# Giving the last 512 rows of a weight matrix to eight of the sixteen DMA engines, and storing the result with one DMA

## The chip, the cores and the metric

The kernel runs on one core of one Trainium2 chip. The metric is the time of one launch on the device, in microseconds (us). The executions of the kernel before lie between 122.95 and 123.44 us in all rounds of the record, and every kernel here was timed beside runs of the kernel before on the same chip. "Span" is the time from the first to the last instruction in the profile; in the kernel before it is about 2 us shorter than the time of the launch.

The profile shows five engines of the core (PE for matmuls, DVE, ACT, POOL, and SP, which here only issues DMAs) and the busy share of its sixteen DMA engines, which move data between the chip's main memory and the on-chip memory SBUF. The kernel uses SBUF as 128 partitions. The second-last load of w_o leaves sixteen completion records in the trace (113.54 to 116.70 us), a store of 8 rows leaves eight (119.60 to 119.68 us) and one more from its issue (118.94). So a `dma_start` is read here as spread over several DMA engines, with one record for the part that one engine carries, called a *share*.

## The reference

The reference is one decoding step for a batch of 8 rows. The input is normalised, and two branches run on the same normalised rows: attention over the last 1024 positions of a cache, and a feed-forward network (FFN). Their results are multiplied and added to the input:

```python
x  = A_x                                   # 8 x 1 x 512, bf16
xn = layernorm(x)
s  = attention(xn, k_cache, v_cache, wq) @ wo       # wo is 4096 x 512
g  = silu((gelu(xn @ w_gate) * (xn @ w_up)) @ w_down)  # w_gate, w_up 512 x 1792; w_down 1792 x 512
return x + s * g
```

Every weight and every cached row is read once, 47.5 MB in all. The arithmetic for 8 rows is small.

## The kernel before

SP issues all loads in one order: the caches and w_q, then w_gate, w_up, w_down, and at the end w_o in four blocks. Every one of these loads writes all 128 partitions. Of the last block, the last quarter is a DMA of its own, so the load that closes the kernel is small.

```python
# w_down: 1792 rows = 128 partitions x 14 rows, two loads of 7 rows a partition
JF = F // P                                   # 14
JH = JF // 2
wd = B_w_down.rearrange("(p j) d -> p j d", j=JF)
for a in range(2):
    t = slot()[:, 0 : JH * D].rearrange("p (j d) -> p j d", j=JH)
    nc.sync.dma_start(out=t, in_=wd[:, a * JH : (a + 1) * JH, :])
...
for m in range(NM):                           # w_o, four blocks of 1 MB
    load_wo(m, cut=HS if m < NM - 1 else HS - 2)   # the last one in 6/8 and 2/8
```

The FFN finishes before the last blocks of w_o arrive. The result sits in PSUM as four column groups of 128; group `q` has the 8 rows of the batch on partitions 32q to 32q+7. Four small DMAs store it, two issued by SP and two by ACT:

```python
def project_out(m):
    for e in range(HS):                       # 8
        for q in range(NQ):                   # 4
            nc.tensor.matmul(s_ps[32 * q : 32 * q + B, :], oE[m][:, e, :],
                             wo_t[m][:, e, q * P : (q + 1) * P], ...)
...
nc.vector.tensor_tensor(out=tmp, in0=s_ps, in1=g_sb, op=ALU.mult)
nc.vector.tensor_tensor(out=out_sb, in0=tmp, in1=xr_sb, op=ALU.add)
for q in range(NQ):
    eng = nc.sync if q % 2 == 0 else nc.scalar
    eng.dma_start(out=out_flat[:, q * P : (q + 1) * P], in_=out_sb[32 * q : 32 * q + B, :])
```

The softmax here doesn't subtract the row's maximum and nothing guards it: scores larger than these inputs give would overflow.

## Time and profile before

| | before |
|---|---|
| time, median (range, 4 runs) | 123.21 us (123.14 to 123.26) |
| span | 121.1 us |
| last share of the second-last w_o load lands | 116.70 us |
| first store issued | 118.47 us |
| last store lands | 120.29 us |

The page of the kernel before: the span, the mean busy share of the DMA engines in 40 equal slices (in tenths), the GB/s in the same slices, two of the queues (packets, MB, share of the sixteen engines' time), and the shares of the chain of waits that ended last.

```profile
span 121.1 us, 4123 instructions
...
DMA  3999999999999999999999999999999999999820
GB/s 84 387 430 430 430 427 417 419 430 425 425 427 427 425 414 422 430 419 430 425 427 422 422 417 430 422 425 422 425 433 418 422 414 434 416 430 423 341 88 5
...
q1 hardware_dynamic: 6800, 47.46, 93.7%
q8 instruction: 14, 0.23, 0.7%
...
DMA 82%; PE 12%; DVE 2%; SPq 1%; issue 0%
```

The kernel is bound by loading: from the third slice to the 37th the engines move 414 to 434 GB/s. The third-last and second-last slices (341, 88) show that the loads do not end together. Queue q8, which the page labels "instruction", has 14 packets of 16 KB in the whole run.

The end of the chain of waits of the kernel before, in order of time. The columns are the start in us, the duration in us, and what it was.

```profile
98.97 17.74 DMA slot<-in_A_wo_dram
116.70 0.04 issue
116.75 1.05 PE s_ps L383 x31
117.80 0.02 issue
117.82 0.30 DVE tmp L483
118.12 0.02 issue
118.14 0.29 DVE out_sb L485
```

So the second-last load of w_o sets the time: when it has landed, at 116.70 us, only about 1.8 us of work and the stores remain. The timeline around it (start in us, length in us, engine, line, what was written and read, and in brackets the idle time before and what ended it):

```profile
108.52 1.12 PE L437 MATMUL m_ps<-slot,hT_sb 128*8 128x128 bf16 x56 [0.55 <-DVE m_ps L433]
...
116.75 1.02 PE L383 MATMUL s_ps<-slot,oE_2360 128*8 128x128 bf16 x32 [0.88 <-DMA slot<-in_A_wo_dram]
...
118.47 0.71 SPq L488 DMA_DIRECT2D out_dram<-out_sb  x2
118.47 0.65 ACTq L488 DMA_DIRECT2D out_dram<-out_sb  x2
```

The completion records say more than the landing time of the whole load. These are the sixteen of the second-last load of w_o, before the change, in us; the trace does not name the engine of a record:

```
113.54 113.55 113.57 113.58 113.77 113.85 114.14 114.42 | 114.97 115.00 | 116.42 116.50 116.53 116.65 116.67 116.70
```

Eight shares end early, two about 1 us later, six about 2.5 us later. That is the opportunity that the change is after. It can be read together with queue q8: each of the 14 instruction packets takes about 0.94 us in its packet record (0.88 to 0.97). Against the mean of the eight early records (113.80 us) the two are 1.2 us late and the six 2.8 us. If an instruction packet sets the later shares of one engine back by 1.2 to 1.4 us, six shares set back twice and two set back once make 14. That is an estimate from these counts.

### The profile page before, as it was taken

To read this page: it belongs to the slowest core of one execution; us is meant where nothing else is said; L and a number is where in the kernel's file an instruction comes from. 1 tells how busy PE (TensorE), PEld (TensorE's weight loads), DVE (VectorE), ACT (ScalarE), POOL (GpSimd) and SP (SyncE) were. 2 spreads that over 40 slices of the span, in tenths; PEclk is the share of its full clock that TensorE was granted. 3 is DMA by queue.
4 is the path that set the end of the run, shared out by engine and by line. 5 is a ranking of instruction groups with operands and counts; after the bars stand their busy time and mean duration, and the time that the engine had idled before them with its cause. 6 is when DMAs were issued, how large, how long until landed. Compare 5 with 4: busy or idle time off the path is not lost.

```text
span 121.1 us, 4123 instructions
## 1 busy us (share of the span) xinstructions
PE 86.0 (71%) x1856; PEld 71.1 (59%) x1856; DVE 72.3 (60%) x150; ACT 22.6 (19%) x70; POOL 2.4 (2%) x15
## 2 busy tenths in 40 slices
PE   0075269696875968999997969566798789955450
PEld 0061029586865957999896969565698542134340
DVE  2352046866956749678989987747798670562000
ACT  0440000321303301212330330303033300300000
POOL 6100000000000000000000000000000000000000
PEclk9999756999999985559999999999999756995555
DMA  3999999999999999999999999999999999999820
GB/s 84 387 430 430 430 427 417 419 430 425 425 427 427 425 414 422 430 419 430 425 427 422 422 417 430 422 425 422 425 433 418 422 414 434 416 430 423 341 88 5
DMA packets 6929, 47.73 MB, mean 394 GB/s; under 512 B 888, under 2 KB 896, under 8 KB 1920
## 3 DMA queue, kind: packets, MB, share of 16 engines
q1 hardware_dynamic: 6800, 47.46, 93.7%
q8 instruction: 14, 0.23, 0.7%
q10 hardware_dynamic: 112, 0.02, 0.1%
q14 instruction: 3, 0.02, 0.1%
HBM read 47.46 MB, written 0.01 MB: 392 GB/s over the span
## 4 chain that ended last, share of the span: by engine, by line
DMA 82%; PE 12%; DVE 2%; SPq 1%; issue 0%
DMA slot<-in_A_k_cache_dram 44%; DMA slot<-in_B_w_gate_dram 16%; DMA slot<-in_A_wo_dram 15%; DMA slot<-in_A_wq_dram 7%; PE kT_ps L282 7%; PE m_ps L329 2%; PE sc_ps L294 2%; SPq L91 1%; PE s_ps L383 1%; DVE kT L286 1%; PE m_ps L316 1%; DVE sums L318 1%; SPq L103 0%; PE m_ps L370 0%; DVE tmp L483 0%
## 5 line engine op out<-in xcount | busy, mean ns | idle before, releaser
L286 DVE COPY kT<-kT_ps 128x1024 bf16<-128x1024 bf16 x64 | 42.2, 677 | 18.1 <-PE kT_ps L282 17.5
L282 PE MATMUL kT_ps<-ident,slot 128*128 128x128 bf16 x512 | 43.4, 234 | 9.9 <-DMA slot<-in_A_k_cache_dram 9.5
L282 PEld LDWEIGHTS <-slot 128*128 128x128 bf16 x512 | 32.6, 104 | 13.3 <-DMA slot<-in_A_k_cache_dram 10.1
L304 ACT ACTIVATE pT<-sc_ps,diag 128x128 bf16<-128x128 f32 x64 | 18.2, 368 | 70.6 <-PE sc_ps L294 70.6
L294 PE MATMUL sc_ps<-qT_all,kT 128*128 128x16 bf16 x512 | 22.9, 171 | 0.3 <-issue 0.3
L329 PE MATMUL m_ps<-pT,slot 128*128 128x16 bf16 x512 | 21.8, 170 | 1.2 <-issue 1.1
L329 PEld LDWEIGHTS <-slot 128*128 128x128 bf16 x512 | 18.6, 97 | 4.6 <-issue 3.1
L294 PEld LDWEIGHTS <-kT 128*128 128x128 bf16 x512 | 20.4, 99 | 0.0
L318 DVE TENSOR_REDUCE sums<-m_ps 128x16 f32<-128x512 f32 x16 | 10.9, 684 | 1.2 <-PE m_ps L316 1.2
L402 PE MATMUL m_ps<-slot,xpT_sb 128*32 128x512 bf16 x32 | 7.7, 1105 | 0.0
L316 PE MATMUL m_ps<-pT,ones_pp 128*128 128x512 bf16 x16 | 6.7, 416 | 0.7 <-ACT pT L304 0.7
L250 PE MATMUL m_ps<-slot,xnT_sb 128*32 128x512 bf16 x32 | 3.5, 527 | 4.2 <-DMA slot<-in_A_wq_dram 4.2
L234 PE MATMUL m_ps<-ident,xhat 8*128 8x8 bf16 x4 | 0.3, 168 | 7.0 <-DVE xhat L214 7.0
L259 DVE CAST q_sb<-m_ps 128x512 bf16<-128x512 f32 x2 | 1.3, 686 | 6.6 <-PE m_ps L250 6.6
L356 DVE TENSOR_TENSOR wide<-m_ps,hmask 64x1024 bf16<-64x1024 bf16 x4 | 4.9, 1216 | 0.5 <-PE m_ps L352 0.4
L483 DVE TENSOR_TENSOR tmp<-s_ps,g_sb 128x128 f32<-128x128 f32 x1 | 0.3, 292 | 7.1 <-PE s_ps L383 7.1
L250 PEld LDWEIGHTS <-xnT_sb 128*32 128x32 bf16 x32 | 0.8, 101 | 6.2 <-issue 5.8
L322 DVE RECIPROCAL recip<-sums 128x16 f32<-128x16 f32 x16 | 4.0, 253 | 0.6
L234 PEld LDWEIGHTS <-xhat 8*128 8x128 bf16 x4 | 0.2, 102 | 7.0 <-DVE xhat L214 7.0
L402 PEld LDWEIGHTS <-xpT_sb 128*32 128x32 bf16 x32 | 1.7, 117 | 4.3 <-issue 3.4
L338 DVE TENSOR_TENSOR oT_all<-m_ps,recip 128x16 bf16<-128x16 f32 x16 | 3.5, 218 | 0.4 <-PE m_ps L329 0.3
L352 PE MATMUL m_ps<-ident,oT_all 128*64 128x128 bf16 x4 | 1.0, 253 | 2.7 <-DVE sums L318 2.1
(71 smaller groups left out, 33.4 us busy)
## 6 DMA issues: line engine op xcount, KB each, us to landing
slot<-in_A_k_cache_dram SPq DMA_DIRECT2D x16, 1024.0 KB, 19.4
slot<-in_A_v_cache_dram SPq DMA_DIRECT2D x16, 1024.0 KB, 19.7
slot<-in_A_wq_dram SPq DMA_DIRECT2D x4, 1024.0 KB, 8.6
slot<-in_A_wo_dram SPq DMA_DIRECT2D x3, 1024.0 KB, 18.0
slot<-in_B_w_gate_dram SPq DMA_DIRECT2D x2, 896.0 KB, 20.0
slot<-in_B_w_up_dram SPq DMA_DIRECT2D x2, 896.0 KB, 18.9
slot<-in_B_w_down_dram SPq DMA_DIRECT2D x2, 896.0 KB
slot<-in_A_wo_dram SPq DMA_DIRECT2D x1, 768.0 KB, 17.7
```

Of the source, the lines that this page charges most:

```text
L250: nc.tensor.matmul(q_ps[n][Q * q : Q * (q + 1), :], xnT_sb[:, k, :], wq_t[k][:, hkv * NW : (hkv + 1) * NW], start=(k == 0), stop=(k == NDC ...
L282: nc.tensor.transpose(t_ps[:, c * P : (c + 1) * P], k_t[g][:, cc * Dh : (cc + 1) * Dh], ident)
L286: nc.vector.tensor_copy(out=kT[n], in_=t_ps)
L294: nc.tensor.matmul(sc[g][:, s * CB + c, :], kT[n][:, c * P : (c + 1) * P], qT_all[:, hkv, b0 : b0 + I, :], start=True, stop=True,)
L304: nc.scalar.activation(out=pT[g][:, :, i * rep : (i + 1) * rep], in_=sc[g][:, :, i * rep : (i + 1) * rep], func=ACT.Exp, bias=diag[:, i : ...
L316: nc.tensor.matmul(sums_ps, ones_pp, pT[g], start=True, stop=True)
L318: nc.vector.tensor_reduce(out=sums, in_=sums_ps.rearrange("p c m -> p m c"), axis=AX.X, op=ALU.add)
L322: nc.vector.reciprocal(out=recip[g], in_=sums)
L329: nc.tensor.matmul(oT[g], v_t[g][:, c * Dh : (c + 1) * Dh], pT[g][:, c, :], start=(c == 0), stop=(c == C - 1),)
L338: nc.vector.tensor_tensor(out=oT_all[:, hkv * rep : (hkv + 1) * rep, b0 : b0 + I].rearrange("p j i -> p i j"), in0=oT[g].rearrange("p (i j ...
L356: nc.vector.tensor_tensor(out=wide, in0=t_ps.rearrange("p (q e) -> p e q", e=HS) .unsqueeze(2) .to_broadcast([HS * B, HS, HS, DQ]), in1=hm ...
L402: nc.tensor.matmul(gu_ps[w][Q * q : Q * (q + 1), :], xpT_sb[:, k, :], cols[:, j0[q] : j0[q] + JQ, :], start=(k == 0), stop=(k == NDC - 1), ...
```

## The change

The intent has two parts. First, the engines that end early should carry more: w_down's last 512 rows go to partitions 0 to 63 alone (the "narrow" load), and the first 1280 rows, 10 for each partition, to all 128. The author reckoned with eight engines for it; its nine completion records in the trace after (one from the issue at 93.34 us, eight from engines at 107.92 to 113.47 us) agree with that.

The trace numbers no DMA engine. Numbers are only names here: engines 0 to 7 are those that carry a load of eight shares (the narrow load, a load of 8 rows), 0 to 3 those that carry a load of four shares, and 8 to 15 the rest of the sixteen. That all loads of eight shares take the same eight engines is an assumption of the author; the records of probe_k and lean256 below fit it.

Second, the rows of the result are laid out 4 partitions apart (row b of group q on partition 32q + 4b), so that one DMA can store everything instead of four.

The diff, cut to its core:

```diff
-        JH = JF // 2
-        wd = B_w_down.rearrange("(p j) d -> p j d", j=JF)
+        JH = JW // 2                                   # JW = 10
+        wd = B_w_down[0:F1, :].rearrange("(p j) d -> p j d", j=JW)      # F1 = 1280
         for a in range(2):
             t = slot()[:, 0 : JH * D].rearrange("p (j d) -> p j d", j=JH)
             nc.sync.dma_start(out=t, in_=wd[:, a * JH : (a + 1) * JH, :])
+        t = slot()[0:PN, 0 : JN * D]                   # PN = 64, JN = 8
+        nc.sync.dma_start(
+            out=t,
+            in_=B_w_down[F1:F, :].rearrange("(y x j) d -> x y (j d)", x=NX, j=JN),   # NX = 8
+        )
 ...
-        oE[m] = persist.tile([P, HS, B], BF16, name=f"oE{m}")
-        nc.vector.tensor_copy(out=oE[m], in_=e_ps)
+        nc.vector.tensor_copy(out=oE[m][:, :, ::QB], in_=e_ps)           # QB = 4; zeros between
 ...
-                    s_ps[32 * q : 32 * q + B, :],
+                    s_ps[Q * q : Q * (q + 1), :],
 ...
-    for q in range(NQ):
-        eng = nc.sync if q % 2 == 0 else nc.scalar
-        eng.dma_start(
-            out=out_flat[:, q * P : (q + 1) * P], in_=out_sb[32 * q : 32 * q + B, :]
-        )
+    nc.sync.dma_start(
+        out=out_flat.rearrange("b (q n) -> q b n", n=P), in_=out_sb[::QB, :]
+    )
```

Left out: the matmuls of the feed-forward network follow the new split (each group of 32 partitions takes 448 hidden columns instead of 512, in two matmuls; h is transposed in six pieces instead of four, and the second product has 72 matmuls instead of 56), the copy of x used for the last addition is loaded by one DMA in the same 4-apart layout, and some memsets of accumulators go away.

More of the change, by code (lines that the diff above doesn't have):

```diff
@@ L53 @@
     SLOT = C * Dh
-    JF = F // P
     NQ = D // P
-    JQ = 4
     Q = 32
+    JW, JN, NX = 10, 8, 8
+    PN = P // 2
+    F1 = JW * P
+    assert F1 + JN * PN == F
+    wide_j = [(0, 3), (3, 6), (6, 8), (8, 10)]
+    narrow_j = [(0, 1), (1, 2), (2, 5), (5, 8)]
+    FQ = F // NQ
     front = ctx.enter_context(tc.tile_pool(name="front", bufs=1))
@@ L74 @@
     ctx.enter_context(tc.manual_schedule())
+    QB = Q // B
     x_flat = A_x.flatten_outer_dims()
@@ L122, in load_ffn @@
             wd_t.extend(t[:, j, :] for j in range(JH))
+        t = slot()[0:PN, 0 : JN * D]
[3 more added lines that the diff above has]
+        )
+        wd_t.extend(t[:, j * D : (j + 1) * D] for j in range(JN))
     HS = SLOT // D
@@ L199 @@
     nc.gpsimd.memset(xq_sb, 0.0)
-    for q in range(NQ):
-        nc.scalar.dma_start(
-            out=xq_sb[32 * q : 32 * q + B, :], in_=x_flat[:, q * P : (q + 1) * P]
-        )
+    nc.scalar.dma_start(out=xq_sb[::QB, :], in_=x_flat.rearrange("b (q n) -> q b n", n=P))
     stats = persist.tile([B, nc.vector.BN_STATS_DIM], FP32, name="stats")
@@ L224 @@
     oT_all = persist.tile([P, Hq, B], BF16, name="oT_all")
-    hT_sb = persist.tile([P, JQ, P], BF16, name="hT_sb")
+    hT_sb = persist.tile([P, 3, P], BF16, name="hT_sb")
+    hN_sb = persist.tile([PN, 3, P], BF16, name="hN_sb")
     g_sb = persist.tile([P, P], FP32, name="g_sb")
     s_ps = ps_s.tile([P, P], FP32, name="s_ps")
-    nc.vector.memset(s_ps, 0.0)
     def transpose_x():
@@ L239, in transpose_x @@
         nc.vector.tensor_copy(out=xnT_sb[:, :, 0:B], in_=t[:, 0])
-        nc.vector.tensor_copy(out=xpT_sb[:, :, 0:B], in_=t[:, 1])
+        nc.vector.tensor_copy(out=xpT_sb[:, :, ::QB], in_=t[:, 1])
     def project_q():
@@ L345, in value_block @@
             )
-    oE, wide_t = {}, {}
+    wide_t = {}
+    oE = [persist.tile([P, HS, Q], BF16, name=f"oE{m}") for m in range(NM)]
+    for m in range(NM):
+        nc.gpsimd.memset(oE[m], 0.0)
     def expand_out(m):
@@ L390, in project_out @@
                 )
-    j0 = [min(q * JQ, JF - JQ) for q in range(NQ)]
     def ffn_up():
-        gu_ps = [ps_m.tile([P, JQ * P], FP32, name="m_ps") for w in range(2)]
+        gu_ps = [ps_m.tile([P, FQ], FP32, name="m_ps") for w in range(2)]
         for w, wt in enumerate((wg_t, wu_t)):
             for k in range(NDC):
-                cols = wt[k // 2][:, k % 2, :].rearrange("x (p j) -> x j p", j=JF)
+                cols = wt[k // 2][:, k % 2, :]
+                wide_c = cols[:, 0:F1].rearrange("c (p j) -> c j p", j=JW)
+                narrow_c = cols[:, F1:F].rearrange("c (y x j) -> c j x y", x=NX, j=JN)
                 for q in range(NQ):
-                    nc.tensor.matmul(
-                        gu_ps[w][Q * q : Q * (q + 1), :],
-                        xpT_sb[:, k, :],
-                        cols[:, j0[q] : j0[q] + JQ, :],
-                        start=(k == 0),
-                        stop=(k == NDC - 1),
-                        skip_group_check=True,
-                    )
-        shape = [P, JQ * P]
+                    dst = gu_ps[w][Q * q : Q * (q + 1), :]
+                    (w0, w1), (n0, n1) = wide_j[q], narrow_j[q]
+                    nw = (w1 - w0) * P
+                    for first, d, c in (
+                        (True, dst[:, 0:nw], wide_c[:, w0:w1, :]),
+                        (False, dst[:, nw:FQ], narrow_c[:, n0:n1]),
+                    ):
+                        nc.tensor.matmul(
+                            d,
+                            xpT_sb[:, k, :],
+                            c,
+                            start=(k == 0 and first),
+                            stop=(k == NDC - 1),
+                            skip_group_check=True,
+                        )
+        shape = [P, FQ]
         zT, uT = gu_ps
@@ L425, in ffn_up @@
         nc.vector.tensor_tensor(out=h_sb, in0=z2, in1=uT, op=ALU.mult)
-        h_ps = ps_m.tile([P, JQ, P], BF16, name="m_ps")
-        for c in range(JQ):
+        h_ps = ps_m.tile([P, 6, P], BF16, name="m_ps")
+        for c in range(3):
             nc.tensor.transpose(h_ps[:, c, :], h_sb[:, c * P : (c + 1) * P], ident)
-        nc.vector.tensor_copy(out=hT_sb, in_=h_ps)
+        for c in range(3):
+            f0 = 2 * P + c * PN
+            nc.tensor.transpose(h_ps[0:PN, 3 + c, :], h_sb[:, f0 : f0 + PN], ident)
+        nc.vector.tensor_copy(out=hT_sb, in_=h_ps[:, 0:3, :])
+        nc.vector.tensor_copy(out=hN_sb, in_=h_ps[0:PN, 3:6, :])
     def ffn_down():
         f_ps = ps_m.tile([P, P], FP32, name="m_ps")
-        nc.vector.memset(f_ps, 0.0)
-        for j in range(JF):
-            r = j // JQ
+        h_col = []
+        for r, (w0, w1) in enumerate(wide_j):
+            h_col += [hT_sb[:, j - w0, Q * r : Q * (r + 1)] for j in range(w0, w1)]
+        for r, (n0, n1) in enumerate(narrow_j):
+            c0 = 3 - (n1 - n0)
+            h_col += [
+                hN_sb[:, c0 + j - n0, Q * r : Q * (r + 1)] for j in range(n0, n1)
+            ]
+        for j in range(JW + JN):
             for q in range(NQ):
                 nc.tensor.matmul(
-                    f_ps[Q * q : Q * q + B, :],
-                    hT_sb[:, j - j0[r], Q * r : Q * r + B],
+                    f_ps[Q * q : Q * (q + 1), :],
+                    h_col[j],
                     wd_t[j][:, q * P : (q + 1) * P],
                     start=(j == 0),
-                    stop=(j == JF - 1),
+                    stop=(j == JW + JN - 1),
                     skip_group_check=True,
@@ L485 @@
     nc.vector.tensor_tensor(out=out_sb, in0=tmp, in1=xr_sb, op=ALU.add)
-    for q in range(NQ):
-        eng = nc.sync if q % 2 == 0 else nc.scalar
-        eng.dma_start(
-            out=out_flat[:, q * P : (q + 1) * P], in_=out_sb[32 * q : 32 * q + B, :]
-        )
+    nc.sync.dma_start(
+        out=out_flat.rearrange("b (q n) -> q b n", n=P), in_=out_sb[::QB, :]
+    )
 _INS = ['A_x', 'A_k_cache', 'A_v_cache', 'A_wq', 'A_wo', 'B_x', 'B_w_gate', 'B_w_up', 'B_w_down']
```

## The prediction

It was written before anything of the change was built or run.

> **What bounds it now.** Loading. The DMA row of the 40 slices stands at 9 from 3 to 112 us, queue q1 moves 47.46 MB, and DMA is 82% of the chain of waits. The end of the chain: the second-last load of w_o lands at 116.70 us, 31 matmuls on s_ps take 1.05 us, two DVE steps 0.6 us, and four stores are issued from 118.47 us.
>
> The last slices (341, 88, 5 GB/s) show a ragged end. By the sixteen completion records that each DMA leaves in the trace, the shares of the second-last load end at 113.54 to 114.42 us (eight), 115.0 (two) and 116.4 to 116.70 (six). The queue table has 14 instruction packets of 16 KB, about 0.94 us each in the packet records; each sets one share back by about 1.2 us, so 6x2 + 2x1 = 14: they fall on eight engines only. [...] Eight engines idle 2 to 3 us at the end while six finish.
>
> **What the change does.**
> 1. w_down: each engine carried 112 KB; now engines 0 to 7 carry 80 + 64, engines 8 to 15 80. With packet times of the trace (8 KB 306 ns start to start, 7 KB about 270, 5 KB about 195 estimated) engines 8 to 15 lose 16 x 75 ns = 1.2 us and engines 0 to 7 gain about 1.25 us. Second-last load: early eight to at most 115.7 us, late six to 115.5. The gate moves from 116.70 to about 115.7: -1.0 us, all on the critical path.
> 2. Store: the four stores land at 119.68, 119.89, 120.09 and 120.29 us, the span ends at 121.1. One DMA should land near 119.8 on the old clock: -0.45 us, all critical. [...]
> 3. PE and DVE: gate/up go from 32 matmuls of 512 columns to 64 with 448 columns per pair; down from 56 to 72 matmuls; transposes from 4 to 6; DVE elementwise 12% shorter; two memsets gone. The FFN ends at 110.6 us, and three w_o blocks (1.02 us each, now waiting 1.4 us each on DMA) follow: several us of slack. Worth 0.
> 4. Start: fewer x issues, four more memsets on POOL: 0.
>
> **Prediction: 121.75 us**, 80% range 121.2 to 123.0. Faster by over 2%: 0.04; within 2%: 0.93; slower by over 2%: 0.03.
>
> **What would show it.** Completion records of the second-last load within about 1 us of each other, the latest near 115.7; the last s_ps stretch starting there, still about 1.05 us; one store about 1.3 us from issue to landing; g_sb long before the last w_o load.
>
> **What would make it wrong.** [...] the narrow load would take up to 2.45 us more. The gain of step 1 would be gone: about 123.1 us. I give this 1 in 4. If the delayed engines were 0 to 7, the gate would move 1.2 us later instead.

Its sum is 123.2 us for the kernel before, less 1.0 us (step 1) and 0.45 us (step 2), which makes 121.75 us. (In the trace after, the single store has four share records, 125.83 to 125.88 us; each of the four stores before has eight.) The 2.45 us of the risk are an estimate: eight packets of 8 KB on an engine, 306 ns each by the trace, taking twice their time.

## The result, and the profile after

| | before | after |
|---|---|---|
| time, median (range, 4 runs each) | 123.21 us (123.14 to 123.26) | 129.32 us (127.9 to 130.4) |
| span of the profiled run | 121.1 us | 127.5 us |
| last share of the second-last w_o load | 116.70 us | 122.33 us |
| store issued, to the end of the span | 118.47 to 121.1 us | 124.11 to 127.5 us |

The ratio of the fast runs is 1.0458, with a 95% interval of 1.0369 to 1.0548. Ratios here are the mean time of one kernel's fast runs over that of the other's of the same rounds, so they are not quite the ratio of the medians. The change makes the kernel slower by 4.6%, and much less even from run to run. The profiled run is the slowest of the four and counts as slow by the rule of 1.5% above the fastest run. Its granted clock, 0.882, is not lower than that of the three others (0.825 to 0.857), so the spread belongs to the kernel.

The page of the kernel after, the same rows as above:

```profile
span 127.5 us, 4222 instructions
...
DMA  3999999999999999999999999999999999999400
GB/s 113 378 422 427 429 429 424 417 434 419 427 422 424 422 424 424 429 417 427 422 427 429 416 427 419 427 424 422 425 425 419 425 313 232 260 381 393 164 16 5
...
q8 instruction: 14, 0.23, 0.6%
```

The two rows must be read together. The engines are as busy as before until the end: the busy row has its nines. But from the 33rd slice on (about 102 us) the rate falls from 425 to 313, 232 and 260 GB/s and comes back late. The engines are busy and move little because their packets take longer, as the packet records below show (a median of 516 ns instead of 309 for the stretched ones of 8 KB). One stretch of the windows view says it in one line; the columns are the stretch and its length, the busy time and count of PE, PE's weight loads, DVE, ACT and POOL, the granted clock, the DMA engines' busy share, and the GB/s. First the kernel before:

```profile
102.00:112.00 10.00, 7.22 (x120) 2.92 (x113) 4.29 (x11) 1.50 (x3) 0.00 (x0) 0.84 1.01 425
```

And after:

```profile
102.00:112.00 10.00, 5.95 (x88) 3.04 (x81) 3.48 (x8) 1.13 (x2) 0.00 (x0) 0.78 1.03 271
```

The DMA share is 1.0 in both, and the rate is 425 against 271 GB/s. The chain of waits and the timeline of the kernel after show what the delay does:

```profile
101.01 21.32 DMA slot<-in_A_wo_dram
122.33 0.04 issue
122.37 1.07 PE s_ps L400 x32
...
123.79 0.29 DVE out_sb L518
```

```profile
113.51 1.04 PE L470 MATMUL m_ps<-slot,hN_sb 64*32 64x128 bf16 x32 [4.04 <-DMA slot<-in_B_w_down_dram]
115.68 1.04 PE L400 MATMUL s_ps<-slot,oE 128*32 128x128 bf16 x32 [1.12 <-DMA slot<-in_A_wo_dram]
...
124.11 0.63 SPq L519 DMA_DIRECT2D out_dram<-out_sb  x1
```

The chain ends exactly as before, with the same 1.05 to 1.07 us of matmuls and the same two DVE steps, but the load of w_o that gates it takes 21.32 us instead of 17.74 and was issued 2 us later. PE waits 4.04 us for the narrow load of w_down. The FFN's new form is not the cause: it waits for data.

The packet records of queue q1 between 92 and 124 us, counted. A packet is called stretched when it took over 12 ns more than the usual time of its size (309 ns for 8 KB, 196 ns for 5 KB); the excess is the sum of the time above the usual.

```
                 8 KB packets   stretched   excess      5 KB packets   stretched   excess
before               411             0       0.0 us          0
after                475           261      49.8 us        256             70       13.8 us
```

Among the stretched 8 KB packets of the kernel after the median is 516 ns. Together the excess is 63.6 us of engine time. Spread over sixteen engines that would be 4.0 us; the gate moved by 5.6 us, because the excess is not spread evenly.

### The profile page after: what moved, and what is told of

Same layout as the page of the kernel before. It is cut to its first block, busy times and chain, and to the rows that moved or that the text cites. A ratio compares the mean times of both kernels' runs of the same rounds, so it can differ in the third digit from the quotient of the medians.

```text
span 127.5 us, 4222 instructions
## 1 busy us (share of the span) xinstructions
PE 87.8 (69%) x1906; PEld 73.9 (58%) x1906; DVE 72.5 (57%) x149; ACT 22.5 (18%) x70; POOL 3.4 (3%) x19
## 4 chain that ended last, share of the span: by engine, by line
DMA 91%; PE 3%; SPq 2%; issue 0%; DVE 0%
DMA slot<-in_A_k_cache_dram 60%; DMA slot<-in_A_wo_dram 17%; DMA slot<-in_B_w_up_dram 15%; SPq L115 2%; PE kT_ps L297 1%; PE s_ps L400 1%; SPq L103 1%; PE m_ps L331 0%; DVE tmp L516 0%; DVE out_sb L518 0%; PE sc_ps L309 0%; PE m_ps L344 0%; SPq L152 0%
## 5 line engine op out<-in xcount | busy, mean ns | idle before, releaser
L297 PE MATMUL kT_ps<-ident,slot 128*128 128x128 bf16 x512 | 43.4, 234 | 10.6 <-DMA slot<-in_A_k_cache_dram 10.3
L400 PE MATMUL s_ps<-slot,oE 128*32 128x128 bf16 x128 | 4.2, 309 | 4.7 <-DMA slot<-in_A_wo_dram 4.7
L265 PE MATMUL m_ps<-slot,xnT_sb 128*32 128x512 bf16 x32 | 4.2, 619 | 4.3 <-DMA slot<-in_A_wq_dram 4.3
L425 PE MATMUL m_ps<-slot,xpT_sb 128*32 128x192 bf16 (+3 forms) x64 | 7.1, 589 | 0.0
L400 PEld LDWEIGHTS <-oE 128*32 128x32 bf16 x128 | 3.4, 138 | 5.4 <-issue 5.4
L425 PEld LDWEIGHTS <-xpT_sb 128*32 128x32 bf16 x64 | 3.0, 118 | 3.3 <-issue 3.2
```

What stands on the lines that cost most here:

```text
L265: nc.tensor.matmul(q_ps[n][Q * q : Q * (q + 1), :], xnT_sb[:, k, :], wq_t[k][:, hkv * NW : (hkv + 1) * NW], start=(k == 0), stop=(k == NDC ...
L297: nc.tensor.transpose(t_ps[:, c * P : (c + 1) * P], k_t[g][:, cc * Dh : (cc + 1) * Dh], ident)
L400: nc.tensor.matmul(s_ps[Q * q : Q * (q + 1), :], oE[m][:, e, :], wo_t[m][:, e, q * P : (q + 1) * P], start=(m == 0 and e == 0), stop=(m == ...
L425: nc.tensor.matmul(d, xpT_sb[:, k, :], c, start=(k == 0 and first), stop=(k == NDC - 1), skip_group_check=True,)
```

## The experiments

**Theories.** The first, the *placement theory*, is the prediction's own risk: to which partitions the narrow rows go, and in what pieces, stretches the packets of the narrow load and of other loads. As one load of 64 partitions it would do harm, as two loads of 32 partitions to the same places it would not, and on the other 64 partitions it would again. The rivals: the load runs slowly because it uses only eight engines or because of the order of its source rows (*form theory*), and the matmuls and the store explain the rest (*compute and store theory*).

The author came to the placement theory by a picture of which engine writes which partitions. No record in these traces names the engine or the partition of a packet. "own_port" is the label of a run and no more.

### again: the kernel after, unedited

The same kernel run again, to have a fast run's profile and to see the spread.

> The changed kernel once more, unedited, for its spread and a second profile. All theories: 127.5 to 130.5 us, ratio to the kernel before about 1.04 to 1.055; packets of the narrow w_down load stretched to about 640 ns; the last w_o load lands after 120 us in the profile.

It took 128.5 us (126.49 to 128.98, 4 runs), beside 123.14 us (122.95 to 123.34, 7 runs) for the kernel before. In its profile, span 124.9 us, 140 of 474 8 KB packets were stretched (excess 24.1 us), and 72 of 256 5 KB packets (10.6 us); the gating load ended at 119.78 us. Half the excess moved the gate by about half as much, 3.1 us instead of 5.6: the time goes with the stretched packets. Not all of the spread does: the runs of 126.49 and 128.11 us have spans of 124.8 and 124.9 us, so 1.6 us between them lie outside the span and were not traced. Two of the four runs (128.89 and 128.98 us) count as slow by the 1.5% rule, at clocks of 0.902 and 0.879, no lower than those of the other two (0.855 and 0.890).

### own_port: the narrow load as two loads of 32 partitions

The rows go to the same 64 partitions, but in two loads, each meant for eight engines again (a load to 32 partitions has eight share records in lean256 below). Bytes, FFN and store stay as in the kernel after.

```diff
-        nc.sync.dma_start(
-            out=t,
-            in_=B_w_down[F1:F, :].rearrange("(y x j) d -> x y (j d)", x=NX, j=JN),
-        )
+        src = B_w_down[F1:F, :].rearrange("(y z j) d -> z y (j d)", z=2 * NX, j=JN)
+        for h in range(2):
+            nc.sync.dma_start(out=t[32 * h : 32 * (h + 1), :], in_=src[NX * h : NX * (h + 1)])
```

(The order of w_gate's and w_up's columns follows.)

> The narrow load is cut into two loads of 32 partitions, [...] same bytes, same engines, same packet size. [...] packets back to about 309 ns, last two w_o loads land near 115.7 and 116.3 us, and with the single store as it is 122.3 to 123.0 us in all. Rival (a load on only 8 engines, or its source pattern with steps of 64 KB, is slow by itself): still above 126 us with stretched packets.

It took 124.28 us (124.05 to 124.49), ratio to before 1.0095 (1.0073 to 1.0118). One of 474 8 KB packets was stretched. Its GB/s row, windows and the end of its chain of waits:

```profile
GB/s 88 407 414 428 428 428 425 423 425 423 425 425 415 428 417 425 425 425 425 425 425 425 423 425 431 417 428 417 428 419 424 420 414 428 429 427 401 259 12 5
```

```profile
102.00:112.00 10.00, 6.70 (x165) 3.84 (x160) 4.12 (x11) 1.40 (x3) 0.00 (x0) 0.93 1.02 427
```

```profile
103.25 14.42 DMA slot<-in_A_wo_dram
117.68 0.04 issue
117.72 1.07 PE s_ps L401 x32
```

The dip is gone (427 GB/s where the kernel after had 271), and with it about 4 to 5 us. But the time expected under the placement theory was missed by over 1 us: the version is still 1% slower than before, and its gating load ends at 117.68 us, not at 115.7. Its sixteen records:

```
112.30 112.62 113.90 114.72 114.82 114.84 114.87 115.30 115.34 115.40 115.40 115.44 115.45 115.67 116.16 117.68
```

Fifteen shares lie where the prediction wanted them or half a microsecond later, and one is late by 1.5 us.

### other_half: the same two loads, to partitions 64 to 127

This keeps own_port's source order and the number, sizes and order of the DMAs, and changes only the partitions.

```diff
-        t = slot()[0:PN, 0 : JN * D]
+        t = slot()[PN:P, 0 : JN * D]
```

(h's transposed pieces move to the same partitions.)

> own_port with one edit: the narrow rows of w_down lie on partitions 64 to 127. Source, engines (0 to 7), number, size and order of the DMAs stay. [...] narrow packets and those of the other half stretch to about 640 ns, the last w_o loads land 2 us or more later than in own_port, and it takes 126 us or more. Rival (source pattern, or eight engines as such): as own_port, 124.0 to 124.5 us, packets of 309 ns.

It took 129.35 us (128.81 to 129.68), ratio 1.0499 (1.0478 to 1.0519). 224 of 473 8 KB packets were stretched, with an excess of 63.9 us. Its GB/s row and the wait for the narrow load:

```profile
GB/s 85 415 425 415 420 433 428 420 425 423 430 415 430 418 428 428 418 430 420 420 428 425 420 430 418 430 420 423 432 417 425 415 329 214 228 289 427 284 31 5
```

```profile
113.70 1.04 PE L471 MATMUL m_ps<-slot,hN_sb 64*32 64x128 bf16 x32 [3.06 <-DMA slot<-in_B_w_down_dram]
```

The same two loads from the same source are fast on one half of the partitions (1 of 474 8 KB packets stretched) and slow on the other (224 of 473). The form theory falls: what counts is to which partitions the rows go, and in what pieces. The placement theory fits. How the place acts is not shown: no record in the trace names a partition or an engine.

The harm is also wider than the prediction had it. Of the packets of 8 and 5 KB that started between 104 and 113 us, all 301 in the kernel after and all 259 in other_half were stretched, at a DMA busy share of 1.0. So the eight engines that carry nothing of the narrow load were slowed too: it has 64 packets, so at least 237 of the 301 belong to other loads, which have sixteen shares. Between 112.45 and 113.0 us in the kernel after, when seven of the narrow load's eight shares had landed, 25 of 26 packets still took 322 to 364 ns instead of 309. After 113.0 us 8 KB packets took their usual time again (none of 156 up to 117 us was stretched), and the eighth share landed at 113.47. The runs show which load does the harm and how to avoid it; how it reaches all sixteen engines stays open.

### wd_as_before: w_down as in the kernel before, the rest of the change kept

This keeps the rows 4 partitions apart, the one load of x and the one store.

```diff
-        wd = B_w_down[0:F1, :].rearrange("(p j) d -> p j d", j=JW)
+        wd = B_w_down.rearrange("(p j) d -> p j d", j=JF)
 ...  (no narrow load; the FFN's matmuls as before)
```

> w_down loaded and used as in the kernel before; rows 4 partitions apart, one load of x and one store kept. If only the narrow load costs: loads land as before (116.7 and 117.3 us). The trace after shows 3.3 us from the issue of the store to the end against 2.67 us before, so I expect 123.5 to 124.0 us, slower than before by 0.3 to 0.8 us. As I predicted the store (saves 0.45 us): 122.7 us. Rival that the store or the row layout explain the loss: above 126 us.

It took 123.88 us (123.82 to 123.95), ratio 1.0062 (1.0046 to 1.0079). So the store part alone costs 0.7 us, where the prediction had it gain 0.45. The loads ended as before (116.65 us). The store in its timeline, and its span:

```profile
118.42 0.69 SPq L486 DMA_DIRECT2D out_dram<-out_sb  x1
```

```profile
span 121.7 us, 4119 instructions
```

The store was issued at 118.42 us, its first completion record from an engine came at 120.16 and the last at 120.22, and the span ended at 121.7. From the issue to the last landing it took 1.80 us, and the four stores of the kernel before took 1.82. So one store is no faster than four: its issue lasts 0.69 us instead of about 0.35 us for one of the four, and its first packet starts 1.29 us after the issue instead of 0.79. And from the landing to the end of the span it took 1.51 us, where the kernel before needed 0.85. What SP does at the end, from the trace:

```
before                                          wd_as_before
118.47, 118.88 stores issued (semaphores        118.42 store issued (semaphore 101)
       106, 108; ACT's have 105, 107)           119.17 wait for 103
119.22 wait for semaphore 103                   119.23 wait for 104 and 101 (lasts 1.01 us)
119.28 wait for 104 and 101                     120.29 wait for 105 and 99
       SP runs nothing for about 0.4 us                SP runs nothing for about 0.4 us
119.73 wait for 105 and 99                      120.75 wait for 107 and 100
119.90 106 and 100, 120.11 107 and 110          120.84 109 and 108, 120.91 110 and 106
120.31 108 and 109                              
120.38 and on: closing steps, alike in both     120.98 and on: closing steps
121.1  end                                      121.7  end
```

At its end the program waits for the semaphore of every DMA, one after the other. In the kernel before the stores' semaphores come late in this order, so the first waits, and a stretch of about 0.4 us in which SP runs nothing (there it may also be the wait for 105, whose last record came at 119.68 us), pass while the stores are under way. The single store took a semaphore that is waited for second, and all the rest came after its landing.

### Three runs on the store: store_adjacent, store_act, wd_as_before_4st

All three start from wd_as_before. The first reads 32 adjacent partitions instead of every fourth (relative error 1.09). Its output is wrong, which doesn't matter for the time.

```diff
-    ... in_=out_sb[::QB, :]
+    ... in_=out_sb[0:Q, :]
```

> wd_as_before with the one store reading partitions 0 to 31 in place of every fourth partition; the result is wrong on purpose. If stepping over partitions makes the store slow: DMA instruction back from 0.65 to about 0.4 us, first packet about 0.8 us after issue in place of 1.3, 0.4 to 0.6 us faster than wd_as_before, so 123.3 to 123.5 us. If the cost is that of a store with four rows per quarter on only 4 engines: 123.8 to 124.0 us as wd_as_before.

It took 124.0 us (123.8 to 124.1), ratio 1.0063. The issue lasted 0.79 us. Stepping over partitions is not what makes the single store slow.

The second issues the same store from ACT instead of SP.

> wd_as_before with its one store issued from ACT in place of SP. If the loss of wd_as_before sits in SP's own instructions after the store (a stall of 0.45 us and five more waits that run only after the landing, 1.48 us from the landing to the end against 0.85 before): most of it is now behind the landing, 0.3 to 0.5 us faster than wd_as_before, 123.4 to 123.6 us. If it sits in the store's own path: 123.8 to 124.0 us.

It took 123.9 us (123.74 to 123.97), ratio 1.0056: no change. The issue lasted 0.61 us, and the store again took semaphore 101, so the closing waits still came after the landing. The engine that issues does not matter here.

The third stores with four DMAs, as before, but from rows 4 apart (`out_sb[Q * q : Q * (q + 1) : QB, :]`).

> wd_as_before with four stores on two queues, each reading every fourth partition of its quarter; 14 instruction fetches as before, so none falls on the stores. If stepping over partitions makes an issue long (0.70 us in own_port_4st against 0.30 to 0.37 us before): four issues of 0.7 us, last landing 2.3 to 2.6 us after the first issue, 123.9 to 124.5 us. If those were long only because an instruction fetch ran at that time: as the kernel before, 123.0 to 123.3 us.

It took 124.57 us (124.49 to 124.68), ratio 1.0112. Each of the four issues lasted 0.64 to 0.79 us, and the last landing came 2.86 us after the first issue, against 1.82 before. For the small stores, stepping over partitions does lengthen the issue; together with store_adjacent this says that an 8-row store of adjacent rows is issued in about 0.35 us here and the other two forms in about twice that. Why was not tested further.

### own_port_4st: own_port with four stores again

> own_port with four stores on two queues in place of one. If the single store costs 0.6 us as the trace of after suggests: 0.4 to 0.8 us below own_port, so 121.7 to 122.4 us, and the fastest of these runs. If the single store saves 0.45 us as I predicted: 0.45 us above own_port.

The edit is the same as in the run before, on top of own_port. It was a miss: I had expected 121.7 to 122.4 us, and it took 125.48 us (124.78 to 125.76), ratio 1.0172 (1.0139 to 1.0205, which leaves the verdict at 2% unclear). The four issues lasted 0.66 to 0.89 us, and a fifteenth instruction packet, at 120.05 us, fell among the stores (this program has about 100 more instructions than the kernel before, whose page has 14 such packets); the last store landed at 123.15 us. The loads ended late as well, at 117.99 us, with one late share. Four stores of rows 4 apart did not help.

### store_sem: the single store with another semaphore

Six tiny DMAs from ACT in mid-kernel, so that the store takes a semaphore that is waited for last.

```diff
+    spare = persist.tile([B, 6, 32], BF16, name="spare")
+    def turn_semaphores():
+        for i in range(6):
+            nc.scalar.dma_start(out=spare[:, i, :], in_=x_flat[:, 32 * i : 32 * (i + 1)])
 ...
+        if n == 40:
+            turn_semaphores()
```

> wd_as_before with six tiny loads more on ACT in mid-kernel, whose only use is that the store takes a completion semaphore six places on in the round. If the 0.7 us are SP's closing waits (the store's semaphore is waited for second, and a stall of 0.45 us and further waits follow the landing): now it is among the last, the end comes about 0.9 us after the landing in place of 1.5, 123.1 to 123.4 us. If the store's own path costs it: 123.8 to 124.0 us as wd_as_before.

It took 123.56 us (123.47 to 126.51, one of the four runs slow; 123.1 to 123.4 was expected), ratio of fast runs 1.0028 (1.0011 to 1.0045).

```profile
span 121.5 us, 4125 instructions
```

```profile
118.83 0.70 SPq L494 DMA_DIRECT2D out_dram<-out_sb  x1
```

From the issue to the end of the span it took 2.65 us, about what the kernel before takes with four stores (2.67), and wd_as_before took 3.31. The 0.66 us of the closing waits are thereby found. (The loads ended 0.35 us later than before, at 117.05; that the tiny DMAs disturbed the queue is likely and was not traced. That is why the time is not quite that of before.) Stored well, one DMA is as good as four, and not better.

### probe_k: which engines do the instruction packets fall on?

This tests the other step of the prediction, that engines 8 to 15 are the delayed ones. Three tiny loads of 8, 4 and 2 rows are appended behind the last load of w_o, in the kernel before. They have 8, 4 and 2 share records. A share's record comes when its engine is through with what it had before, as the records below are read, so they show how late these engines are.

```diff
+    probe = persist.tile([B, 3, D], BF16, name="probe")
+    for i, rows in enumerate((8, 4, 2)):
+        nc.sync.dma_start(out=probe[0:rows, i, :], in_=x_flat[0:rows, :])
```

> The kernel before with three tiny loads of 8, 4 and 2 rows queued behind the last w_o load[...]. From own_port I expect among the lowest 8: six near 114.2 to 115.1 us and two 1.2 us or more later, so that set-back engines are not only 8 to 15; by my prediction's reading all eight would be early. The loads of 4 and 2 rows tell which of the eight the two are.

("The lowest 8" there are the engines of the load of 8 rows, called 0 to 7 here.)

The one run (124.57 us; its time is of no interest) had these records:

```
last load of w_o, 16 engines: 114.08 114.10 114.11 114.15 114.30 114.40 114.69 115.16 115.54 115.56 117.06 ... 117.25
8 rows, engines 0 to 7:       114.28 114.29 114.33 114.52 114.87 115.35 115.75 115.76
4 rows, engines 0 to 3:       114.47 114.51 115.05 115.53
2 rows, engines 0 and 1:      114.65 115.22
```

The two shares that were set back once (115.54 and 115.56 in the first row) appear as 115.75 and 115.76 among the eight, and nowhere among the four (the last at 115.53). None of the eight is as late as the six shares from 117.06 us on. So the instruction packets fall on eight engines, as the prediction said, but by this reading on six of 8 to 15 and on two of 4 to 7. The numbers are the names given above: the two are on engines of the load of 8 rows and, if the load of 4 rows takes four of these eight, not on those.

The durations of the instruction packets repeat with a period of eight, and with them the dealing can be followed in the other traces. These are the packets of the kernel before, in ns, in order:

```
935 933 922 960 967 947 879 879 | 936 931 922 967 960 949
```

The seventh and eighth of each round, at 879 ns, are taken to be the two on engines 4 to 7: in this run they occur once each, and the other six twice each, which is the 6 x 2 + 2 x 1 of the records. Where the round starts is not fixed. The kernel after started at the fifth packet of the round in its profile and at the second in the run "again", the same program. In own_port the round started at the second, and a seventh-of-the-round packet (881 ns) fell at 111.8 us, by this reading on an engine of 4 to 7 that had had one already and carried the narrow load's extra bytes: this is taken to be the late share at 117.68 us. What sets the start of the round stays open.

So giving more bytes to engines 0 to 7 cannot bring the full gain, even where no packet is stretched: two of the eight get one or two instruction packets as well (one each in the kernel before, two each in lean256).

### Smaller doses: lean256, lean256_pad, lean256_act, lean256_sem

With these I looked for a version that beats both kernels. All start from the kernel before, with its stores, and give only 256 rows to engines 0 to 7, as two loads of 32 partitions to partitions 0 to 63.

```diff
+    JW, JN, NX, PN = 12, 4, 8, P // 2
-        wd = B_w_down.rearrange("(p j) d -> p j d", j=JF)
+        wd = B_w_down[0:F1, :].rearrange("(p j) d -> p j d", j=JW)
+        src = B_w_down[F1:F, :].rearrange("(y z j) d -> z y (j d)", z=2 * NX, j=JN)
+        for h in range(2):
+            nc.sync.dma_start(out=t[32 * h : 32 * (h + 1), :], in_=src[NX * h : NX * (h + 1)])
```

> The kernel before, with its stores, its row layout and nearly its count of PE instructions (16 more rows), and only 256 rows of w_down on partitions 0 to 63, in two loads of 32 partitions[...]. My theory: engines 8 to 15 lose 0.6 us and engines 0 to 7 gain 0.6; the latest of the second-last w_o load moves from 116.7 to 116.1 us; two of engines 0 to 7 also get instruction fetches, one each within the span as in the kernel before. 122.5 to 122.7 us, faster than before by 0.4 to 0.5%. Rival (uneven loads never help since fetches fall on both halves alike): 123.1 us or more.

It was a miss: expected 122.5 to 122.7 us, measured 124.35 us (123.41 to 124.6, 6 runs), ratio 1.0087 (1.0063 to 1.011).

```profile
117.01 0.04 issue
117.05 1.05 PE s_ps L392 x32
```

```profile
118.77 1.06 SPq L500 DMA_DIRECT2D out_dram<-out_sb  x2
118.77 0.66 ACTq L500 DMA_DIRECT2D out_dram<-out_sb  x2
```

The gating load ended at 117.01 us: the round had started at the fifth packet, so by the reading above both engines among 4 to 7 had two instruction packets before it (the narrow load's first half has the records 104.25 to 105.17 for six shares, and 107.15 and 107.20 for these two). And SP needed 1.06 us for its two stores instead of 0.71, because a stretch in which it ran nothing fell between them; the store issued last had semaphore 101, which is waited for second, and one of its shares was late (121.41 us, the others by 120.80).

lean256_pad adds 48 transposes that nothing uses, to have a fifteenth instruction packet and another dealing.

> lean256 with 48 transposes more on PE after the FFN, written to a tile that nobody reads: 3,826 PE rows as in the changed kernel, which had a 15th instruction fetch. If the count of fetches decides which engine gets the late ones: 15 fetches, one engine of 0 to 7 gets two before the loads end, its last w_o share lands at about 117.0 us, 123.2 to 123.8 us and more spread than lean256. Rival [...]: as lean256 within 0.15 us.

It took 125.03 us (124.14 to 126.31), ratio 1.0139. The expectation, 117.0 us for the gate because one of engines 0 to 7 would get two packets, failed: in its profile, by the round of durations, no engine of 4 to 7 had two packets in time, and the gating load ended at 115.96 us, 0.74 us before that of the kernel before. That is the gain the prediction had in mind, in one profile. It did not reach the end: the padding held PE from 112.20 to 115.72 us, so that the blocks of w_o came late, PE then stood idle for another 0.84 us that the trace puts down to no wait, and the first store was issued at 119.35 us, 0.88 us later than in the kernel before.

lean256_act issues the narrow load from ACT in mid-kernel into a tile of its own, and drops a set of transposes to keep the number of instructions down.

> lean256 with the narrow loads issued by ACT in mid-kernel into a tile of their own and without the second set of x transposes: PE rows 3,722 and SP rows as in the kernel before. If lean256 lost 0.5 us through a stall of SP between its stores: stores end as before, 0.4 us or more below lean256. With the instruction fetches dealt as in the kernel before (two engines of 0 to 7 get one each): last shares of the second-last w_o load at 116.1 us and 122.5 to 122.8 us, faster than before. With two on one of them: 117.0 us and 123.3 to 123.8 us.

It took 123.78 us (122.66 to 123.93), ratio 1.0022 (0.9992 to 1.0053). The six runs, 123.84, 123.82, 122.66, 123.93, 122.91 and 123.73 us, lie on two levels about 1 us apart; the profile fell on the upper one (gating load at 117.03 us). Two levels are what a dealing that changes from run to run would give; the lower level was not profiled, so this is argued and not shown.

lean256_sem adds the six tiny DMAs of store_sem.

> lean256_act with the same six tiny loads, so that its stores take late semaphores as in the kernel before. By the closing waits: 0.4 to 0.6 us below lean256_act in each of its two levels: about 123.2 us where an engine of 4 to 7 gets two instruction fetches and the narrow load, about 122.2 us where none does. If the closing waits don't matter: 123.8 and 122.8 us.

It was spoiled: 126.08 us (126.0 to 126.84). The DMA rate fell to 192 and 190 GB/s in the slices at about 71 to 78 us. That ACT's tiny loads share semaphores with SP's loads (as ACT's loads of x do in the kernel before: 105, 106, 107 and 99) is the likely cause; it was not shown. Its tail from issue to end, 2.69 us, was as short as meant.

### Engines 0 to 3 alone: four_engines, four_engines_sp, four_engines_fit

If engines 0 to 3 get no instruction packets (in probe_k none of the four records comes after 115.53 us), they are the right ones for the extra bytes. 256 rows go to partitions 0 to 15 and 32 to 47, in two loads of 16 partitions and four blocks of rows; that these go by engines 0 to 3 alone is the author's assumption. The first attempt issued this from ACT:

> The same 256 rows on partitions 0 to 15 and 32 to 47[...]; stores as in lean256_sem. If fetches on two of engines 4 to 7 took the gain: engines 4 to 15 lose 0.6 us, 0 to 3 gain 1.8 us; second-last w_o load complete at 116.1 to 116.4 us in every run, one level, 122.6 to 122.9 us, faster than before by 0.3 to 0.5%. Rival (uneven loading gains nothing, whichever engines carry it): 123.1 us or more.

It took 150.37 us and says nothing about the engines: ACT stood idle for 33.45 us, until 117.47 us, which the trace puts down to the landing of ACT's tiny loads. The second issues it from SP:

```diff
-    JW, JN, NX, PN = 12, 4, 8, P // 2
+    JW, JN, NX, PN = 12, 8, 4, P // 2
-                out=t[32 * h : 32 * (h + 1), :], in_=src[NX * h : NX * (h + 1)]
+                out=wdn[32 * h : 32 * h + 16, :], in_=src[NX * h : NX * (h + 1)]
```

> As lean256 (both narrow loads from SP, four stores), but the 256 rows go to partitions 0 to 15 and 32 to 47 by engines 0 to 3. If fetches on two of engines 4 to 7 set lean256's slow level (its latest share of the second-last w_o load at 117.0 us): here the latest share is at 116.1 to 116.5 us and the runs have one level, 0.4 to 0.8 us under lean256's 124.35, so 123.5 to 124.0 us; SP's stall between the stores stays, so not faster than the kernel before. If uneven loading gains nothing whichever engines carry it: 124.2 us or more, latest share at 117 us.

It took 123.8 us (123.64 to 124.51, 6 runs), ratio 1.006 (1.004 to 1.008).

```profile
span 122.0 us, 4204 instructions
```

```profile
116.36 1.06 PE L397 MATMUL s_ps<-slot,oE 128*8 128x128 bf16 x32 [0.90 <-DMA slot<-in_A_wo_dram]
118.11 1.07 SPq L522 DMA_DIRECT2D out_dram<-out_sb  x2
```

The gate moved earlier in this version too, to 116.32 us (before: 116.70), and five of the six times lie within 0.31 us. But the stores took 3.84 us from the first issue to the end of the span instead of 2.67: SP's two issues took 1.07 us again, and the store issued last again had semaphore 101, with a share that landed at 120.88 us: the second closing wait lasted until then, and all the others followed. The last version adds six tiny loads to SP's own queue, early in the kernel, to put the semaphores right.

> four_engines_sp with six tiny loads among SP's loads, so that the stores take the semaphores that they have in the kernel before and SP's stall falls before its first store. If closing waits and stall are the rest: from the first store's issue to the end about 2.7 us in place of 3.9, loads complete as in four_engines_sp (116.3 us), 122.6 to 122.9 us, faster than the kernel before by 0.2 to 0.5%. If uneven loads cost something after the loads themselves: 123.4 us or more.

It took 122.65 us (122.46 to 124.87, 6 runs) beside 123.06 us (123.04 to 123.34, 11 runs), ratio 0.9979 (0.9943 to 1.0016). Four of the six runs, 122.46 to 122.68 us, are 0.3 to 0.5% faster than before. Their granted clocks are 0.877 to 0.914. Two, with 0.834 and 0.835, are slower, 124.87 and 124.05. The profile fell on one of these:

```profile
116.20 3.54 PE s_ps L401 x128
```

In it PE ran all four blocks of w_o in one stretch, to the end at 119.74 us, though the gating load had landed at 116.34 us and the last at 117.0: here PE sets the time. That the extra matmuls of this version leave PE no slack when its clock is low fits this profile and the two clocks; it was not tested. The span ends 2.67 us after the first store's issue. So the landing and the tail behave as designed, and a gain of 0.4 to 0.6 us is there in four runs of six, but a version that beats the kernel before is not established.

## Why the prediction was wrong

The prediction was 121.75 us with a range of 121.2 to 123.0 and a chance of 0.03 for "slower by over 2%"; the measured 129.32 us is 6.1 us slower than before.

**What bounds the kernel: right.** The second-last load of w_o gates the end in both kernels; the work behind it kept its 1.05 to 1.07 us.

**"They fall on eight engines only": right. That all eight are among 8 to 15: wrong for two of eight.** Two are among 4 to 7 (probe_k). I had generalised from two packets. The consequence is the late share of own_port: the gate at 117.68 us instead of 115.7.

**"-1.0 us" in step 1: wrong, and this is the step that failed most.** It rests on packets of the narrow load taking their usual time. They do not, and neither do the packets around them: the narrow load has only 64 packets of 8 KB, and 261 of that size were stretched, so at least 197 of them belong to w_o. The prediction named the risk, gave it "1 in 4" and sized it "up to 2.45 us more" for the narrow load, 123.1 us in all. That size took the narrow load by itself: eight engines at 2.45 us are 19.6 us of engine time. Measured were 63.6 us in the profile of the kernel after and 34.7 in that of "again". The prediction charged the eight engines of the narrow load alone; from 104 to 113 us the packets of all sixteen were stretched, with 70 of the 5 KB packets of the wide w_down loads among them, and the gate moved to 122.33 us. With the term replaced, own_port is 5.0 us faster than the kernel after and 4.2 us faster than "again", of losses of 6.1 and 5.4 us. That the place and the pieces of the narrow rows are the cause is shown (1 of 474 8 KB packets stretched in own_port, 224 of 473 in other_half); how they act is not.

**"-0.45 us" in step 2: wrong in sign.** The store part alone costs 0.7 us (wd_as_before). The prediction costed the landing and took the end of the span to follow at once. The landing came no earlier (1.80 against 1.82 us after the issue), because the issue itself is longer, and the program's closing waits, which the four stores had hidden, came after it: 1.51 us instead of 0.85 (store_sem brings it back to 0.85).

**Steps 3 and 4, compute and start, "worth 0": right.** In own_port, which has all of the new compute, the matmuls of the FFN end before the w_o blocks arrive, and PE waits for DMA before each of the three last blocks. They are not quite free, though: with some 100 more instructions than the kernel before a fifteenth instruction packet comes close to the end of the run, and in own_port_4st, at 120.05 us, it fell on the stores.

In short sums: own_port is at +1.1 us against the kernel before. In its profile the span is 1.3 us longer: the gate is 1.0 us later, by the dealing followed above probably because of an instruction packet on an engine of 4 to 7, and the end from the store's issue is 0.3 us longer (3.01 us instead of 2.67; its store had semaphore 104, and the 0.7 us of wd_as_before are not all there). The other 4 to 5 us are the stretched packets. The spread of 126.49 to 130.4 us between runs of one program goes in part with the number of stretched packets (140 and 261 in the two profiles); what makes them more or less frequent was not settled.

## What to carry to other kernels

When a load covers only part of the partitions, compare the packet times of all loads around it with their usual time, and try the load in other pieces and places: here, from 102 to 112 us, two loads of 32 partitions moved 427 GB/s where one load of 64 brought everything down to 271, and the same two loads on the other 64 partitions to 250. A DMA busy share of 1.0 with a falling rate was its sign here, and it slowed every engine, not only those of the load that caused it (all 301 packets of 8 and 5 KB from 104 to 113 us). Before moving bytes between DMA engines, see how late each group of engines ends (tiny loads of 8, 4 and 2 rows behind the last load did it here), because the instruction packets were dealt unevenly (by the records before, six engines had two and two had one), and differently from run to run (two runs of the kernel after began at the fifth and at the second packet of the round). And cost the end of a kernel to the last wait of the program, not to the landing of its last store: here the closing waits were worth 0.66 us.
